# Three of a decode kernel's fourteen weights loads issued as parts of their rows

## The chip, the cores and the metric

One core of a Trainium2 chip runs the whole program. The metric is the device time of one execution in microseconds (us); the time before is 2493.15 us, the median of two runs (2493.1 and 2493.21).

## The reference

Two tokens (batch 2, one query position, width 512) go through four blocks: attention, mixer, attention, mixer, each with a residual sum around it. Both attention blocks use the same weights and the same caches.

```python
q = (x @ wq).reshape(B, Sq, 32, 128)              # 32 query heads, 8 key/value heads
scores = einsum("bhqd,bhkd->bhqk", q, k) * Dh**-0.5   # k, v: 2 x 8 x 32768 x 128 f32
o = einsum("bhqk,bhkd->bhqd", softmax(scores), v)
x = x + o.reshape(B, Sq, 4096) @ wo
h = layernorm(layernorm(x)); u = gelu(einsum("bsd,sf->bdf", h, w1) + b1)   # f = 1792
x = x + transpose(einsum("bdf,fs->bds", u, w2) + b2)
```

For one batch entry and one key/value head the keys are 16 MB and the values 16 MB. There are 16 such pairs and two layers, so nearly all the data that has to be read is the two caches, twice.

## The kernel before

The work is cut into 32 units: a layer, a batch entry and a key/value head. A unit reads its keys in eight chunks of 128 x 4096 floats (2 MB each), multiplies each by the queries into `scores` (`k_chunk`, L418), takes the maximum and the exponentials, then reads its values in eight chunks and sums them up in `acc` (`v_chunk`, L563). Small steps close the unit: denominators, the output projection into `rows` (`add_row`, L236), and after the last unit of a batch entry the mixer.

All large transfers are issued by SyncE on one queue (SP), in one order that is written out when the program is built: the list `stream`, sorted by a key that interleaves the keys of a unit with the values of the unit before. Except around the change of layers, a transfer brings four chunks, 8 MB (128 rows of 64 KB). The target is one large SBUF tile `mem`, divided into 13 cells of 128 x 4096 floats (16 KB in each of 128 partitions). Nine cells form the ring for keys and values, so a transfer is issued only when TensorE has finished with the cells it overwrites. Four cells hold weights.

The weights of a head are one row of `wqo`: for each of 128 partitions 8 KB of `wq` and 8 KB of `wo`, 2 MB in all, contiguous in HBM. `load_weights` (L113 to L115) brings them with one transfer of 128 rows of 16 KB. Fourteen such loads are made: all eight heads in the first layer (order 0, 1, 2, 3, 4, 6, 5, 7, `passing` ahead of `RESIDENT`) and again the six heads of `passing` in the second. Each is booked ten chunks ahead of its unit's first key chunk (L908, `at(kbeg[n] - 10, load_weights, ...)`); the first product that reads them (`q_products`, L330) is booked six chunks ahead of it.

Around the change of layers (roughly from 1010 to 1560 us of the span) transfers are smaller, 256 KB to 4 MB, because the units of heads 5 and 7 of both layers are interleaved with the mixer, and some chunks stay in SBUF for the second layer.

The builder gives every transfer of the two hardware queues one of eight semaphores in turn. A transfer adds to its semaphore as its data lands, and a reader waits for the semaphores of all transfers that bring what it reads.

Of the kernel before, what the change touches and what calls it, by code (L numbers as in the profile page):

```python
# [13 lines left out]
P = 128  # L14
# [21 lines left out]
DIRECT = 2  # L36
TAIL_GROUPS = (3, 3, 3, 2, 1)
IDLE = (4, 1, 3, 2)
EPS = 1e-5


@with_exitstack
def gqa_mixer_kernel(ctx: ExitStack, tc: tile.TileContext, x, kt, v, wqo, cols, out):
# [17 lines left out]
    nc = tc.nc  # L61
# [42 lines left out]
    def cells(k, m=1):  # L104
        return mem[:, k * CK : (k + m) * CK]
# [4 lines left out]
    def wo_at(h):  # L110
        return cells(home[h])[:, W:].rearrange("p (t c) -> p t c", t=R)

    def load_weights(h, cell):  # L113
        home[h] = cell
        nc.sync.dma_start(cells(cell), wqo[h])  # L115


    busy = [0] * 2 * (WCELL0 + WCELLS + 1)
# [57 lines left out]
    booked, closed = {}, {}  # L176

    load_weights(0, WCELL0)
    cols_sb = sm["cols"]
    nc.scalar.dma_start(cols_sb, cols)  # L180
# [64 lines left out]
    def first_input():  # L245
# [13 lines left out]
        nc.vector.tensor_reduce(rs, p[:, : B * DT].rearrange("p (b d) -> p b d", b=B), axis=AX.X, op=ALU.add)  # L259
        nc.vector.tensor_scalar(rs, rs, 1.0 / D, EPS, op0=ALU.mult, op1=ALU.add)  # L260
        nc.gpsimd.tensor_tensor(rs, rs, half_neg.to_broadcast([P, B]), op=ALU.pow)
# [49 lines left out]
    def unit_of(n):  # L311

        return units[n]
# [320 lines left out]
    def deviation(dst, mv):  # L634


        nc.vector.tensor_scalar(dst, mv[:, 1:2], 1.0 + EPS, EPS * EPS, op0=ALU.mult, op1=ALU.add)
        nc.gpsimd.tensor_tensor(dst, dst, half_neg, op=ALU.pow)
# [49 lines left out]
    def idle_products(k):  # L688


        p = misc()
        for _ in range(k):
            nc.tensor.matmul(p[:, :P], ident, ident, start=True, stop=True)

    def last_mixer(n):
# [21 lines left out]
        for k in range(2):  # L717
# [3 lines left out]
            nc.vector.bn_stats(st[:, k, :], halves[k][:, :w])  # L721
        idle_products(IDLE[0])
        nc.vector.bn_aggr(mv, st)
# [8 lines left out]
        for g in range(NG):  # L732
# [7 lines left out]
            )  # L740
        idle_products(IDLE[1])

        def project(f):
            for g in range(NG):
                nc.tensor.matmul(  # L745
                    kept[0][32 * g : 32 * g + 1, :P],
                    w2z[:, f, 1:],
                    tiles[f][:, g * P : (g + 1) * P],
                    start=False,
                    stop=(f == FT - 1),  # L750
                    skip_group_check=True,
                )

        for f in range(DIRECT):
# [3 lines left out]
            project(f)  # L758
        idle_products(IDLE[2])
        f0 = DIRECT  # L760
        for i, m in enumerate(TAIL_GROUPS):
# [8 lines left out]
            if i < 2:  # L770
                idle_products(IDLE[3])
            f0 += m
# [45 lines left out]
    def statistics(key):  # L818
# [3 lines left out]
        nc.vector.bn_aggr(mv, st)  # L822
        nc.vector.tensor_scalar_add(rs, mv[:, 1:2], EPS)
        nc.gpsimd.tensor_tensor(rs, rs, half_neg, op=ALU.pow)
# [43 lines left out]
    kbeg, k_done, vbeg, v_done, brings, t = {}, {}, {}, {}, [], 0  # L868
# [9 lines left out]
    def at(time, f, *a, rank=1):  # L878
        done.setdefault(time, []).append((rank, f, a))

    HC = NCH // HALVES
    weight_cell = {h: WCELL0 + h % WCELLS for h in heads}
    again = dict(zip(passing, (WCELL0 + k for k in (0, 2, 3, 1, 0, 2))))
    mixed = {}
    for n in range(NU):
        layer, b, h = unit_of(n)
# [18 lines left out]
            if place is S[0]:  # L905
                assert v_done[n - 2, HC - 1] <= q2
        if n and (units[n] == (0, 0, h) or h in passing and units[n] == (1, 0, h)):
            at(kbeg[n] - 10, load_weights, h, (again if layer else weight_cell)[h])  # L908
        if n in (N1 + 1, N2 + 1):
            at(kend - 0.5, turn_scores, n, 0, rank=2)  # L910
            at(kend, q_products, n + 1, 0)
# [157 lines left out]
```

## Time and profile before

| what | value |
|---|---|
| median of two runs | 2493.15 us |
| the profiled execution's own time | 2494.97 us |
| its span, first to last instruction | 2493.1 us |
| TensorE busy | 1378.2 us (55%) |
| VectorE busy | 240.1 us (10%) |
| ScalarE busy | 187.9 us (8%) |
| moved by DMA | 1063.04 MB, mean 426 GB/s |
| mean granted TensorE clock | 0.771 |

A page of the profile has the busy time of each engine, 40 slices of the span, the DMA queues with the share of the core's 16 DMA engines that they kept busy, the chain of work that ended last, the costliest groups of instructions with what they waited for, and the DMA issues. A table by stretches of time gives the same for chosen windows. PE is TensorE, DVE VectorE, ACT ScalarE, POOL GpSimd, SP SyncE; SPq is SP's queue of issues. No view tells the 16 DMA engines apart; their mean busy share in short stretches is what can be read.

### The profile page before, as it was taken

The page shows a single profiled execution, that of the slowest core. Times are in us where ns is not written, and L with a number is a line of the kernel's source. Part 1 is how long each engine was busy: PE and PEld are TensorE (multiplying, and loading weights), DVE is VectorE, ACT ScalarE, POOL GpSimd, SP SyncE. Part 2 cuts the span into 40 slices and gives each one's busy share as a digit, 9 for nine tenths or more (in the row PEclk, how much of TensorE's full clock was granted, in tenths as well). Part 3 has the DMA queues.
Part 4 walks back from the last instruction along what each step waited for, and adds up shares of the span by engine and source line. Part 5 has one row for each costly group of instructions (what it writes and reads, how often), then busy time and mean ns, then how long its engine had stood idle before and what let it go on. Part 6 is the DMA issues. An engine that isn't in the chain of part 4 may idle for free.

```text
span 2493.1 us, 20496 instructions
## 1 busy us (share of the span) xinstructions
PE 1378.2 (55%) x9270; PEld 369.7 (15%) x9270; DVE 240.1 (10%) x632; ACT 187.9 (8%) x554; POOL 4.9 (0%) x17
## 2 busy tenths in 40 slices
PE   4544554545445554767677665365546555455546
PEld 1111111111111111111121111111111111111112
DVE  1000000000000000003113110000000000010002
ACT  0000000000000000002012010000000000011002
POOL 0000000000000000000000000000000000000000
PEclk7777777877777777778798887777777777777778
DMA  9999999999999999999999999999999999999996
GB/s 420 436 433 424 436 436 433 430 436 433 431 429 437 433 430 431 429 426 403 428 425 421 427 430 427 435 433 428 435 433 433 430 432 432 430 436 431 431 436 282
DMA packets 34080, 1063.04 MB, mean 426 GB/s; under 512 B 4037, under 2 KB 4041, under 8 KB 4938
## 3 DMA queue, kind: packets, MB, share of 16 engines
q1 hardware_dynamic: 33704, 1061.70, 99.1%
q8 instruction: 73, 1.20, 0.2%
q14 instruction: 13, 0.11, 0.0%
q10 hardware_dynamic: 290, 0.04, 0.0%
HBM read 1061.72 MB, written 0.00 MB: 426 GB/s over the span
## 4 chain that ended last, share of the span: by engine, by line
DMA 74%; PE 24%; issue 0%; DVE 0%; ACT 0%; SPq 0%; POOL 0%
DMA mem<-in_v_dram 39%; DMA mem<-in_kt_dram 35%; PE scores L418 11%; PE acc L563 11%; PE kept L330 1%; PE rows L236 1%; PE bcast L330 1%; PE small L603 0%; PE small L447 0%; PE small L594 0%; PE kept L745 0%; PE small L441 0%; PE bcast L813 0%; PE small L356 0%; SPq L136 0%
## 5 line engine op out<-in xcount | busy, mean ns | idle before, releaser
L418 PE MATMUL scores<-mem,small_sb 128*32 128x512 f32 x4096 | 629.9, 732 | 615.9 <-DMA mem<-in_kt_dram 615.8
L563 PE MATMUL acc<-mem,S 128*16 128x512 f32 x4088 | 612.0, 735 | 454.1 <-DMA mem<-in_v_dram 454.1
L418 PEld LDWEIGHTS scores<-mem,small_sb 128*32 128x32 f32 x4096 | 147.8, 128 | 1008.8 <-issue 902.5
L458 ACT ACTIVATE S<-S,small_sb 128x128 f32<-128x128 f32 x240 | 123.5, 518 | 2103.1 <-DVE small_sb L449 1628.4
L563 PEld LDWEIGHTS acc<-mem,S 128*16 128x16 f32 x4088 | 133.3, 110 | 815.5 <-issue 674.0
L433 DVE TENSOR_REDUCE small_sb<-scores 128x1 f32<-128x512 f32 x64 | 44.2, 690 | 826.9 <-PE scores L418 826.9
L453 DVE STREAM_TRANSPOSE S<-scores 128x512 f32<-128x512 f32 x64 | 45.4, 710 | 123.6 <-PE acc L563 123.6
L330 PE MATMUL kept<-mem,small_sb 128*2 128x512 f32 x104 | 50.1, 606 | 1.7 <-DVE small_sb L264 1.7
L236 PE MATMUL rows<-mem,small_sb 128*1 128x512 f32 (+1 forms) x276 | 48.6, 617 | 2.6 <-ACT mem L788 2.4
L458 ACT ACTIVATION_READ_ACCUMULATOR S<-S,small_sb 128x1 f32 x240 | 44.8, 187 | 0.0
L443 DVE TENSOR_REDUCE small_sb<-small 1x4 f32<-1x128 f32 x32 | 8.9, 279 | 287.8 <-PE small L441 287.8
L596 DVE RECIPROCAL small_sb<-small 128x4 f32<-128x4 f32 x32 | 5.9, 184 | 291.9 <-PE small L594 291.9
L605 DVE TENSOR_TENSOR small_sb<-small,small_sb 128x4 f32<-128x4 f32 x31 | 5.1, 164 | 289.4 <-PE small L603 289.4
L533 DVE SCALAR_TENSOR_TENSOR S<-acc,small_sb,S 128x128 f32<-128x128 f32 x93 | 32.6, 351 | 3.3
L788 ACT ACTIVATE S<-bcast,small_sb 128x512 f32<-128x512 f32 x28 | 21.6, 777 | 94.2 <-DVE small_sb L657 92.1
L531 DVE TENSOR_SCALAR S<-acc,small_sb 128x128 f32<-128x128 f32 x31 | 10.8, 349 | 160.0 <-PE acc L563 160.0
L356 PE MATMUL small<-small_sb,mem 2*128 2x2 f32 x112 | 14.7, 249 | 17.9 <-DVE mem L352 17.9
L603 PEld LDWEIGHTS small<-small_sb,S 128*128 128x128 f32 x62 | 12.6, 255 | 46.4 <-issue 39.6
L330 PE MATMUL bcast<-mem,small_sb 128*1 128x512 f32 (+1 forms) x40 | 19.1, 592 | 0.0
L805 DVE SCALAR_TENSOR_TENSOR acc<-S,small_sb,acc 128x512 f32<-128x512 f32 x24 | 18.1, 754 | 2.5
L356 PEld LDWEIGHTS small<-small_sb,mem 2*128 2x128 f32 x112 | 13.5, 186 | 30.5 <-DVE mem L352 27.3
L441 PE MATMUL small<-small_sb 128*1 128x128 f32 x64 | 17.1, 362 | 0.4 <-DVE small_sb L439 0.4
(134 smaller groups left out, 266.9 us busy)
## 6 DMA issues: line engine op xcount, KB each, us to landing
mem<-in_kt_dram SPq DMA_DIRECT2D x32, 2048.0 KB, 16.4
mem<-in_v_dram SPq DMA_DIRECT2D x23, 2048.0 KB, 20.9
mem<-in_v_dram SPq DMA_DIRECT2D x9, 4096.0 KB, 32.0
mem<-in_wqo_dram SPq DMA_DIRECT2D x14, 2048.0 KB, 33.3
mem<-in_kt_dram SPq DMA_DIRECT2D x7, 4096.0 KB, 23.7
mem<-in_kt_dram SPq DMA_DIRECT2D x24, 1024.0 KB, 8.9
mem<-in_v_dram SPq DMA_DIRECT2D x21, 1024.0 KB, 8.1
mem<-in_v_dram SPq DMA_DIRECT2D x2, 1280.0 KB, 26.6
```

What stands on the lines that cost most here:

```text
L236: nc.tensor.matmul(rows[32 * g : 32 * g + b + 1, :], weights if b else weights[:, 1:], row, start=False, stop=True, skip_group_check=True,)
L330: nc.tensor.matmul(q_ps[n][:m, :], xnT[:, d, b : b + m], wq_at(h)[:, d, :], start=(d == 0), stop=(d == DT - 1),)
L356: nc.tensor.matmul(pt[:, r * m : (r + 1) * m], q_row[n][:m, r * DH : (r + 1) * DH], ident[:m, :m], start=True, stop=True,)
L418: nc.tensor.matmul(sc_ps[n, half][32 * g : 32 * g + 32, :], q, kc[k * NG + g], start=(i == 0 and k == 0), stop=(i == PACK - 1 and k == SUB ...
L433: nc.vector.tensor_reduce(mx[n][:, half : half + 1], sc_ps[n, half], axis=AX.X, op=ALU.max)
L441: nc.tensor.matmul(pm[:1, :P], mxa, ident, start=True, stop=True)
L453: nc.vector.transpose(S[half], sc_ps[n, half])
L458: nc.scalar.activation(s[:, :, h], s[:, :, h], AF.Exp, bias=neg[n][:, h : h + 1], scale=SCALE, accum_out=lsum[n][:, half, h : h + 1],)
L533: nc.vector.scalar_tensor_tensor(t, acc[:, k * DH : (k + 1) * DH], mask[:, k : k + 1], t, op0=ALU.mult, op1=ALU.add)
L563: nc.tensor.matmul(acc[32 * g : 32 * g + R * QT, :], S[half][:, col : col + R * QT], vc[q], start=(c == 0 and q < NG), stop=(c == NCH - 1 ...
L788: nc.scalar.activation(hid[key, f], px[key], AF.Gelu_apprx_tanh, bias=shift[key][:, f : f + 1], scale=slope[key][:, f : f + 1],)
L805: nc.vector.scalar_tensor_tensor(h if f == FT - 1 else acc, h, w, acc, op0=ALU.mult, op1=ALU.add)
```

## The change

The first-layer loads of heads 3, 4 and 6 come in parts: three transfers of 112, 8 and 8 rows, two of 120 and 8, and two of 112 and 16. Together they write the same rows to the same cells. The other eleven loads, those of the same heads in the second layer among them, stay whole. Four transfers are added in all. In the order of SP's instructions the parts stand where the whole load stood; the order of the other engines is the same. The first query product of each of the three heads waits for three or two semaphores in place of one, and later transfers get another of the eight semaphores.

```diff
+UNEVEN = {3: (112, 8, 8), 4: (120, 8), 6: (112, 16)}
...
-    def load_weights(h, cell):
+    def load_weights(h, cell, reloaded=False):
         home[h] = cell
-        nc.sync.dma_start(cells(cell), wqo[h])
+        p = 0
+        for m in UNEVEN[h] if h in UNEVEN and not reloaded else (P,):
+            nc.sync.dma_start(cells(cell)[p : p + m, :], wqo[h][p : p + m, :])
+            p += m
...
-            at(kbeg[n] - 10, load_weights, h, (again if layer else weight_cell)[h])
+            at(kbeg[n] - 10, load_weights, h, (again if layer else weight_cell)[h], layer > 0)
```

## The prediction

> **What bounds the kernel now.** I read the page's DMA lines first, then the chain that ended last, then a table by stretches, then the last microseconds slice by slice. From the page:
>
> ```profile
> span 2493.1 us, 20496 instructions
> DMA packets 34080, 1063.04 MB, mean 426 GB/s; under 512 B 4037, under 2 KB 4041, under 8 KB 4938
> q1 hardware_dynamic: 33704, 1061.70, 99.1%
> q8 instruction: 73, 1.20, 0.2%
> DMA 74%; PE 24%; issue 0%; DVE 0%; ACT 0%; SPq 0%; POOL 0%
> L418 PE MATMUL scores<-mem,small_sb 128*32 128x512 f32 x4096 | 629.9, 732 | 615.9 <-DMA mem<-in_kt_dram 615.8
> L563 PE MATMUL acc<-mem,S 128*16 128x512 f32 x4088 | 612.0, 735 | 454.1 <-DMA mem<-in_v_dram 454.1
> ```
>
> SP's queue q1 keeps the 16 DMA engines busy for 99.1% of the span, and both large groups of matmuls are idle for as long as they wait for its data. TensorE is no bound. The 24% of the chain on PE is not time without transfers; the table by stretches shows why (columns: busy us and counts of PE, PEld, DVE, ACT, POOL, granted clock, DMA share, GB/s):
>
> ```profile
> 60.00:380.00 320.00, 162.34 (x1114) 44.77 (x1114) 21.75 (x63) 19.34 (x72) 0.00 (x0) 0.75 1.00 433
> 380.00:720.00 340.00, 172.93 (x1190) 47.15 (x1194) 23.57 (x68) 17.21 (x64) 0.00 (x0) 0.76 1.00 433
> 720.00:1010.00 290.00, 148.43 (x995) 39.83 (x986) 19.57 (x54) 15.01 (x56) 0.00 (x0) 0.75 1.00 431
> 1140.00:1190.00 50.00, 37.60 (x234) 9.36 (x230) 24.13 (x46) 14.12 (x19) 1.09 (x2) 0.88 0.98 396
> 1560.00:2440.00 880.00, 454.87 (x3071) 123.03 (x3063) 65.92 (x184) 64.92 (x197) 0.54 (x1) 0.75 1.00 432
> ```
>
> From 60 to 1010 us the DMA share is 1.00 at 431 to 433 GB/s: the next transfer is always queued. All three changed loads lie there. An edit can move the time only by how long the DMA engines need, and a transfer has landed only when its slowest engine is done. The table is a mean over 16 engines; whether they run level shows where the queue runs dry. The end of the last transfers:
>
> ```profile
> 2470.00:2471.00 1.00, 0.85 (x8) 0.00 (x0) 0.00 (x0) 0.00 (x0) 0.00 (x0) 1.00 1.02 408
> 2471.00:2472.00 1.00, 0.32 (x4) 0.13 (x8) 0.00 (x0) 0.00 (x0) 0.00 (x0) 1.00 0.67 268
> 2472.00:2473.00 1.00, 1.00 (x16) 0.23 (x8) 0.00 (x0) 0.00 (x0) 0.00 (x0) 1.00 0.49 197
> 2473.00:2474.00 1.00, 0.59 (x8) 0.00 (x0) 0.00 (x0) 0.00 (x0) 0.00 (x0) 1.00 0.50 195
> 2474.00:2475.00 1.00, 0.88 (x8) 0.13 (x8) 0.00 (x0) 0.00 (x0) 0.00 (x0) 1.00 0.27 104
> 2475.00:2476.00 1.00, 0.78 (x20) 0.32 (x16) 0.70 (x2) 0.00 (x0) 0.00 (x0) 1.00 0.13 49
> 2476.00:2477.00 1.00, 0.72 (x19) 0.22 (x16) 0.70 (x2) 0.00 (x0) 0.00 (x0) 1.00 0.01 4
> ```
>
> The share falls from 1.0 to 0.5 within 2471 to 2472, rests there for two slices, and then falls to nothing. Read as two halves: 0.67 is 0.50 of one half and 0.17 of the other, which therefore ended about 0.34 us into its slice, at 2471.3; the second half holds 0.50 + 0.49 + 0.50 + 0.27 + 0.13 + 0.01 = 1.90 of half a share, 3.8 us, and ends at 2474.8 on the mean, 3.5 us later. So there is a fast half and a slow half. The same at the end of the first stage:
>
> ```profile
> 1146.00:1147.00 1.00, 1.00 (x9) 0.10 (x9) 0.84 (x3) 0.00 (x0) 0.00 (x0) 1.00 0.94 393
> 1147.00:1148.00 1.00, 0.35 (x2) 0.26 (x2) 0.16 (x1) 0.00 (x0) 0.00 (x0) 1.00 0.65 254
> 1148.00:1149.00 1.00, 0.63 (x8) 0.26 (x12) 0.00 (x0) 0.00 (x0) 0.00 (x0) 1.00 0.95 287
> ```
>
> About a third of the engine time is idle between 1147 and 1148 us. That is where the first stage's lead is given up, because the next issue waits for data from the slow half. The instruction packets fit as the cause: 0.2% of 16 engines over 2493.1 us is 80 us (60 to 100 by the rounding), 1.1 us for each of 73. If they fell on eight engines, the 1560 to 2440 stretch with its 24 would set those back three each, 3.3 us:
>
> ```profile
> q8 instruction: 24, 0.39, 0.2%
> ```
>
> **The change part by part.** *One row.* The 433 GB/s of the 380 to 720 row over 16 engines is 27.06 GB/s each, so a row of 16,384 bytes takes 0.605 us, and a load of 2,097,152 bytes 4.84 us, eight rows an engine. No byte is added.
>
> *Who gets the rows.* 112 rows are seven an engine, 16 rows one. Eight rows cannot reach more than eight engines. If both 8-row parts of head 3 go to the same eight, those have nine rows and the others seven; 120 rows do not go evenly into 16, and with its 8 the load of head 4 gives some engines nine, some eight and at least one fewer. Head 6 stays at eight each. What counts is the most loaded engine of the slow half:
>
> - the eight that are used again are the fast half: the slow ones lose a row with head 3 and none or more with head 4, so the end moves by -0.605 us;
> - they are the slow half: one row more with head 3 and one with head 4, +1.21 us;
> - the two 8-row parts take different halves: head 3 gives 0, head 4 lies between 0 and +0.605 us.
>
> No row of the trace says which half takes short parts. I take -0.605 us: only in that case do the rows laid on the other half cost nothing, as two rows, 1.21 us, lie within the 3.5 us that the fast half is ahead. That the slow half is the one spared is the one step here that rests on judgement. [...]
>
> *Rows that run beside others' rows.* All transfers before are of 128 rows, so no row shows what an odd number does to the engines' rate. Bounds: 0, if a row costs 0.605 us whatever stands beside it; at the other end every row of the three loads at half rate, 3 x 4.84 = 14.5 us. Below nothing is excluded, because no engine can move a row faster than at the steady 1.00 share. I take 0, as in the stretches 60 to 1010 us the rate holds at 431 to 433 GB/s with any mix of key, value and weights rows, and keep 14.5 for the range.
>
> *Four more issues on SP.* One line of the load's source (min, median and max ns of an issue), then the issues in order of time around heads 3 and 6, where they stand between a value load and the next key load:
>
> ```profile
> L115 SPq DMA_DIRECT2D mem<-in_wqo_dram x14: 397/427/1462, 0.7 to 1974.8; - x14
> ```
>
> ```profile
> 379.51 0.33 SPq L136 DMA_DIRECT2D mem<-in_v_dram  x1
> 379.89 1.00 SPq L115 DMA_DIRECT2D mem<-in_wqo_dram  x1
> 400.03 0.33 SPq L136 DMA_DIRECT2D mem<-in_kt_dram  x1
> 700.80 0.44 SPq L115 DMA_DIRECT2D mem<-in_wqo_dram  x1
> 720.93 0.33 SPq L136 DMA_DIRECT2D mem<-in_kt_dram  x1
> ```
>
> An issue takes 0.43 us (1.46 at most). Head 3's two more end near 381.8 us, at most near 384, and the next issue is at 400.03 us, held by its buffer; around head 6 the gap is 20.1 us too, and at 1.46 us each the parts still fit. Cost 0; without that gap it would be 4 x 0.43 = 1.7 us. Later transfers also wait for their semaphore's use eight issues earlier, which is long over: the load of head 3 lands 33.1 us after its issue, and with an issue some 20 us apart eight of them are over 100 us.
>
> *The first query product.* It now waits for the last of three parts. The landing of head 3's load, then its reader:
>
> ```profile
> DMA to landing us min/median/max: 33.1/33.1/33.1
> ```
>
> ```profile
> L330 PE MATMUL kept<-mem,small_sb x8: 592/592/592, 437.6 to 442.3; 128*2 128x512 f32 x8
> ```
>
> The load lands at 379.9 + 33.1 = 413.0 us and is read at 437.6 us, so 24 us of lateness are covered, more than the 14.5 of the upper bound. Behind the product on PE stand score products, which would wait with it only past that. The other two loads are booked at the same distance. Cost 0.
>
> *The sum.* -0.605 us at the end of the first stage, handed on unchanged, as everything after 1148 us starts from landings. The profiled execution took 2494.97 us for a span of 2493.1 and would take 2494.4; it stands 1.8 us over the median, 2493.15 us, from which the forecast is 2492.5 us.
>
> **The rivals.** *Parts that get in each other's way (slower).* The eight rows of a small part go to neighbouring partitions. If four of them share a way into SBUF, they take turns: four rows one behind the other, 2.42 us in place of 0.605, and an engine of the slow half standing among them loses 1.8 us which it never makes up before the queue runs dry, for its share is 1.00. Three loads at one such stall each: +5.4 us, 2498.6 us; the bounds are one stall less the row saved (+1.2, 2494.4) and the half rate, +14.5 (2507.7). It decides as soon as an engine of the slow half loses more than 0.605 us. For it speaks that the rate of 433 GB/s is so steady that something fixed limits it; against it that no stretch shows two transfers slowing each other. [...]
>
> *The slow half is the loaded one.* +1.21 us, 2494.4 us. For it speaks nothing more than for the forecast but the chance of two halves.
>
> *The change does nothing.* The short parts spread so that each half keeps its rows, or the lead is set anew after 1148 us: 2493.15 us. For it speaks the drained stretch 1140 to 1190 us with its share of 0.98; against it that a stage which starts earlier also ends earlier.
>
> **How the numbers follow.** Forecast 2492.5 us, its own range 2491.9 (one row more saved) to 2493.0: 0.44. Parts in each other's way: 0.38. Loaded slow half: 0.10. Nothing: 0.08. The range 2491.9 to 2501.0 leaves out the stalls beyond +7.8 us, a third of that rival (0.13), and some 0.04 below. All cases lie within 2% (50 us; about what a measurement of this kernel can tell from no change): faster by more 0.01, within 0.98, slower by more 0.01, for a mechanism not thought of.
>
> **What would show it.** Right: the 1560 to 2440 and 720 to 1010 rows keep 1.00 and 432 GB/s, the first dry slice comes about 0.6 us before 1147 with a share over 0.65, since the halves are nearer to each other, and the three loads in parts land no later than 33 us after issue. Wrong, by stalls: GB/s of the 380 to 720 row falls (5 us of 340 are 1.5%, some 6 GB/s), the parts land later, and the dry slice comes later than 1147 us. Wrong, by halves: the rate stays, and the dry slice is 1.2 us later and deeper than 0.65.

## The result and the profile after

The changed kernel takes 2522.53 us (median of two runs, 2520.17 and 2524.9) against 2493.15 us: ratio 1.0113, 95% interval [1.0096, 1.0129], 29.4 us slower. The prediction, 2492.5 us in a range of 2491.9 to 2501.0, missed it; its slower rival had the kind of loss right and was too small by a factor of five. The profiled execution took 2520.17 us with a span of 2518.4 us, 25.3 us longer than before.

From the page of the changed kernel, the lines that answer to those shown of before:

```profile
span 2518.4 us, 20504 instructions
DMA packets 34119, 1063.04 MB, mean 422 GB/s; under 512 B 4076, under 2 KB 4080, under 8 KB 4977
q1 hardware_dynamic: 33743, 1061.70, 99.1%
q8 instruction: 73, 1.20, 0.2%
DMA 74%; PE 24%; issue 0%; DVE 0%; ACT 0%; SPq 0%; POOL 0%
mem<-in_wqo_dram SPq DMA_DIRECT2D x2, 1792.0 KB, 41.4
```

The bytes are the same, the queue's share is still 99.1%, and only the mean rate fell, from 426 to 422 GB/s. So the engines do not wait for more work than before; the same work takes longer. The packets under 512 B rose by 39. Before, 60 to 1010 us hold 864 of them for 53 transfers issued there, all of 128 rows, and 400 to 425 us hold 32, around the whole load of head 3 and one other transfer: 16 each. In the changed kernel 48 fall between 400 and 430 us, around the parts of head 3 and one whole transfer, 39 between 569 and 595 us around those of head 4 and another, and 48 between 738 and 765 us around those of head 6 and a third. Less 16 for each whole transfer, the parts leave 32, 23 and 32, together 87 where three whole loads leave 48. They are read here as one for each engine that takes part in a transfer, which no view shows.

By stretches of time (the last two columns are DMA share and GB/s):

```profile
60.00:380.00 320.00, 162.34 (x1114) 44.88 (x1114) 21.72 (x63) 19.32 (x72) 0.00 (x0) 0.75 1.00 433
380.00:720.00 340.00, 167.38 (x1120) 44.98 (x1120) 23.46 (x67) 17.18 (x64) 0.00 (x0) 0.73 1.00 410
720.00:1010.00 290.00, 146.53 (x988) 39.71 (x988) 19.73 (x55) 14.97 (x56) 0.00 (x0) 0.75 1.00 419
1560.00:2440.00 880.00, 460.65 (x3080) 123.92 (x3080) 66.21 (x185) 64.92 (x197) 0.54 (x1) 0.75 1.00 432
```

The rate falls exactly where the changed loads lie: heads 3 and 4 in the 380 to 720 row, head 6 in the next. 340 x (433 - 410) / 433 = 18.1 us and 290 x (431 - 419) / 431 = 8.1 us make 26.1 us, about the 25.3 us by which this execution's span is longer (the rates are rounded to 1 GB/s, so each term is good to within 1 us). In the rows before 380 and after 1560 us the rates are those of before, 433 and 432 GB/s. Around head 3, in slices of 5 us, before:

```profile
405.00:410.00 5.00, 1.73 (x12) 0.44 (x16) 0.00 (x0) 0.00 (x0) 0.00 (x0) 0.50 1.04 446
410.00:415.00 5.00, 5.00 (x42) 1.32 (x38) 0.18 (x1) 0.00 (x0) 0.00 (x0) 0.84 1.12 478
415.00:420.00 5.00, 2.40 (x24) 0.47 (x16) 0.72 (x1) 0.00 (x0) 0.00 (x0) 1.00 0.97 419
```

and after:

```profile
400.00:405.00 5.00, 0.11 (x4) 0.00 (x0) 1.48 (x3) 2.11 (x8) 0.00 (x0) 0.99 0.95 383
405.00:410.00 5.00, 0.00 (x0) 0.00 (x0) 0.00 (x0) 0.00 (x0) 0.00 (x0) 0.50 0.92 216
410.00:415.00 5.00, 4.09 (x20) 0.94 (x24) 0.00 (x0) 0.00 (x0) 0.00 (x0) 0.50 1.30 236
415.00:420.00 5.00, 5.00 (x50) 1.38 (x42) 0.18 (x1) 0.00 (x0) 0.00 (x0) 0.98 0.93 213
420.00:425.00 5.00, 0.49 (x8) 0.00 (x0) 0.72 (x1) 0.00 (x0) 0.00 (x0) 1.00 0.90 383
```

For 15 us the engines are as busy as ever (0.92, 1.30 and 0.93, 1.05 on the mean) and move half: 216, 236 and 213 in place of 433 GB/s. That is the lesson of this profile: a DMA share of 1.00 did not mean here that the packets in flight moved at full rate. The missing rate over 405 to 425 us, 5 x (217 + 197 + 220 + 50) / 433, is 7.9 us for this load.

The loss is not given back. The stretches up to 1140 us hold a share of 1.00 on the mean, and the value transfer that SP issued at 1010.1 us is now issued at 1035.0. From 1040 us on, where the transfers are smaller, the first slice of 1 us with a share under 0.75 comes at 1174 us, not 1147. Ahead of that such slices say nothing: they swing in both runs, as with 0.58 at 404 us before.

```profile
1173.00:1174.00 1.00, 1.00 (x8) 0.11 (x8) 0.89 (x3) 0.00 (x0) 0.00 (x0) 1.00 0.98 410
1174.00:1175.00 1.00, 0.40 (x5) 0.30 (x2) 0.16 (x1) 0.00 (x0) 0.00 (x0) 1.00 0.71 295
```

### The profile page after: what moved, and what is told of

It is laid out like the page before. It is cut to its first block, busy times and chain, and to the rows that moved or that the text cites. A ratio compares the mean times of both kernels' runs of the same rounds, so it can differ in the third digit from the quotient of the medians.

```text
span 2518.4 us, 20504 instructions
## 1 busy us (share of the span) xinstructions
PE 1384.1 (55%) x9270; PEld 370.7 (15%) x9270; DVE 240.3 (10%) x632; ACT 187.9 (7%) x554; POOL 4.9 (0%) x17
## 3 DMA queue, kind: packets, MB, share of 16 engines
q1 hardware_dynamic: 33743, 1061.70, 99.1%
## 4 chain that ended last, share of the span: by engine, by line
DMA 74%; PE 24%; issue 0%; DVE 0%; ACT 0%; SPq 0%; POOL 0%
DMA mem<-in_kt_dram 38%; DMA mem<-in_v_dram 37%; PE scores L422 11%; PE acc L567 10%; PE kept L334 1%; PE bcast L334 1%; PE rows L240 1%; PE small L451 0%; PE small L607 0%; PE small L598 0%; PE kept L749 0%; PE bcast L817 0%; PE small L360 0%; PE small L445 0%; ACT S L462 0%
## 5 line engine op out<-in xcount | busy, mean ns | idle before, releaser
L809 DVE SCALAR_TENSOR_TENSOR acc<-S,small_sb,acc 128x512 f32<-128x512 f32 x24 | 18.1, 755 | 2.5
## 6 DMA issues: line engine op xcount, KB each, us to landing
mem<-in_wqo_dram SPq DMA_DIRECT2D x2, 1792.0 KB, 41.4
```

The costliest lines, as they stand in the source:

```text
L809: nc.vector.scalar_tensor_tensor(h if f == FT - 1 else acc, h, w, acc, op0=ALU.mult, op1=ALU.add)
```

## The experiments

My theory after the result, which no trace had shown, was that of the slower rival, made general: DMA engines that write neighbouring partitions at one time share a way into SBUF, and a part of the rows brings engines together that a transfer of all 128 rows keeps apart (shared ways). The rivals were that the loss comes from uneven row counts, from splitting as such, or from where in HBM the engines read at one time (source). Each variant is the kernel before with an edit of `load_weights`; where nothing else is said, it acts on the first-layer loads of heads 3, 4 and 6. Each was timed beside the kernel before on the same chip.

**Split by columns.**

```diff
+        for f in (0, W) if h in (3, 4, 6) and not reloaded else (None,):
+            a = slice(f, None if f is None else f + W)
+            nc.sync.dma_start(cells(cell)[:, a], wqo[h][:, a])
```

> The same three loads (heads 3, 4, 6, first layer) come as two transfers each, of all 128 rows and half of the columns (8 KB a row). Four theories. Shared ways: DMA engines that write neighbouring partitions at one time share a way into SBUF, which a transfer of all 128 rows avoids; 2493 us, within 1.5. Uneven: the loss comes from DMA engines with more rows than others; 2493 us. Splitting: each added transfer costs something; about 29 x 3/4 = 22 us more, 2515. Source: the loss comes from where in HBM the engines read at one time (7 rows of 16 KB apart in place of 4); 2493 us.

Measured: 2493.99 us beside 2494.21, ratio 1.0 [0.9991, 1.001]. Splitting costs nothing that can be measured, and neither do rows of 8 KB. Splitting falls.

**Two parts of 64 rows.** `for m in (64, 64)`, rows in order.

> The three loads come as 64 and 64 rows: four rows for each of 16 engines, but all within one half of the partitions. Shared ways: rows at about half rate, 4.84 us more for each load, about 2508 us (2503 to 2515). Uneven: rows are even, 2493 us. Splitting: three added transfers, about 2515 us. Source: blocks of four rows as in the whole load, 2493 us.

Measured: 2519.44 us beside 2494.21, ratio 1.0099 [1.0084, 1.0114], 25.2 us more, 8.4 a load. Two parts of the same size, four rows for each of 16 engines if they are spread evenly, and nearly the whole loss: uneven and source both expected none. Shared ways had the sign, but 4.84 us a load was too small.

**Only head 6, 112 and 16 rows.**

> Only head 6 in parts, 112 and 16 rows: seven and one row for each engine, so eight each as before. Shared ways: a third of the loss, about 2502 us (2500 to 2505). Uneven: no loss, 2493 us. Splitting: one of four added transfers, about 2500 us. Source: about 2502 us.

Measured: 2503.98 us beside 2494.21, ratio 1.0038 [1.0025, 1.0051], 9.8 us. In the changed kernel the two parts of this load leave 32 small packets, as many as two whole transfers. So by the reading above all 16 engines have rows of both, seven and one if they are spread evenly, and uneven row counts are not needed for the loss.

**Whole loads from spaced source rows.**

```diff
+        src = wqo[h]
+        if h in (3, 4, 6) and not reloaded:
+            flat = wqo[h : h + 2].rearrange("h p c -> (h p c)")
+            src = flat[: P * 7168].rearrange("(p c) -> p c", c=7168)[:, : 2 * W]
+        nc.sync.dma_start(cells(cell), src)
```

> The three loads stay whole, but their source rows stand 28 KB apart, so that blocks of four rows start 112 KB apart as blocks of seven 16 KB rows do (the weights of the three heads are then others than the reference's). Source: about the whole loss, 2515 to 2523 us. Shared ways, uneven and splitting: 2493 us, within 1.5.

Measured: 2494.15 us beside 2494.21, ratio 0.9998 [0.9989, 1.0008]. Source rows 28 KB apart in place of 16 cost nothing that can be measured. This speaks for the side that is written, but only for whole loads: no part of neighbouring partitions was filled from spaced source rows.

**Which partitions meet.** Two pictures of what engines share, both suppositions that no trace shows, are set against each other. Halves: all partitions below 64 share one way, and all from 64 on another. Small ways: small groups of neighbouring partitions have ways of their own. Four variants vary the rows of a part at even counts: four parts of 32 neighbouring rows; the even and the odd rows; every fourth row; and four parts of 16 neighbouring rows with one of 64. The even and the odd rows are

```diff
+        for k in range(2) if h in (3, 4, 6) and not reloaded else (None,):
+            a = slice(k, None, None if k is None else 2)
+            nc.sync.dma_start(cells(cell)[a, :], wqo[h][a, :])
```

with `range(4)` and a step of 4 for every fourth row; the others are `for m in (32,) * 4` and `for m in (16, 16, 16, 16, 64)` in order of rows.

> The three loads come as four parts of 32 neighbouring rows (0 to 31, 32 to 63, 64 to 95, 96 to 127), two rows for each of 16 engines. Halves (all partitions below 64 share what they write through, and all above): as for 64 and 64 rows, about 2519 us. Small ways (groups of four neighbouring partitions, and the same 32 further, share one way): two engines on each of eight ways throughout, half rate, 2505 to 2530 us; it does not tell the two apart, but splitting, if it mattered, would show against two parts. Nothing shared: 2493 us.

> The three loads come as two parts of 64 rows, the even and the odd ones, so that each part reaches all of the 128 partitions with the same counts as 64 and 64 rows. Halves: engines 0 to 7 stay below partition 64 and the others above, no loss, 2493 to 2496 us. Small ways: each engine has four rows of every second partition, two ways, which it shares with one other engine; half rate, 2508 to 2520 us.

> The three loads come as four parts of 32 rows, every fourth partition. Halves: no loss, 2493 to 2496 us. Small ways: two engines start on the same way, but each engine's second row is on another, so a pair falls out of step and shares only now and then; 2500 to 2513 us, less than the four parts of neighbouring rows.

> The three loads come as four parts of 16 neighbouring rows and one of 64: one row for each of 16 engines four times, then four. Halves (what is shared is one way as wide as eight engines for all partitions below 64): the same as 64 and 64 rows, 8 to 9 us a load, 2519 to 2522 us. Small ways (each group of four neighbouring partitions has one as wide as one engine): 16 rows reach four ways, so four engines share each and a row takes 2.4 us in place of 1.2; 4 x 1.8 + 2.4 us and what the neighbours lose, 13 us a load, about 2533 us.

Measured: 32 neighbouring rows 2521.04 us beside 2494.07, ratio 1.0108 [1.0093, 1.0123]; even and odd rows 2494.3 beside 2494.07, ratio 1.0001 [0.9991, 1.0011]; every fourth row 2494.33 beside 2494.07, ratio 1.0001 [0.9992, 1.0011]; 16 neighbouring rows 2522.06 beside 2495.24, ratio 1.0104 [1.0087, 1.0121]. Halves had all four about right; small ways expected a loss from both strided variants and 2533 us from the 16 neighbouring rows, and missed these three.

One pair carries the study: 64 neighbouring rows and 64 rows at every second partition have the same sizes and the same number of parts, and cost 25.2 us and nothing (2494.3 us beside 2494.07). Slices of 5 us around head 3, first with 64 and 64 neighbouring rows:

```profile
405.00:410.00 5.00, 0.00 (x0) 0.00 (x0) 0.00 (x0) 0.00 (x0) 0.00 (x0) 0.50 0.87 177
410.00:415.00 5.00, 2.63 (x16) 0.68 (x20) 0.00 (x0) 0.00 (x0) 0.00 (x0) 0.50 1.26 269
415.00:420.00 5.00, 5.00 (x42) 1.36 (x38) 0.19 (x1) 0.00 (x0) 0.00 (x0) 0.80 0.97 242
```

then with the even and the odd rows:

```profile
405.00:410.00 5.00, 1.54 (x8) 0.37 (x12) 0.00 (x0) 0.00 (x0) 0.00 (x0) 0.50 1.06 452
410.00:415.00 5.00, 5.00 (x34) 1.34 (x30) 0.04 (x1) 0.00 (x0) 0.00 (x0) 0.64 1.05 449
415.00:420.00 5.00, 3.48 (x32) 0.70 (x24) 0.86 (x2) 0.00 (x0) 0.00 (x0) 1.00 1.03 446
```

Half rate against full rate, at the same share. What decides is which rows a part takes, neighbouring or spaced, not how many rows it has or how many parts there are. The pair does not tell writing from reading: with the partitions the source rows are spaced too. The strided parts had been expected to cost something by small ways, with each engine taking rows next to each other in the list; that picture of which engine writes which rows falls with the 0.2 and 0.3 us measured.

**Each load alone.** Head 3 in (112, 8, 8) and head 4 in (120, 8).

> Only head 3 in parts, 112, 8 and 8. If the loads' losses add up, 7.5 to 8.5 us by the landings behind it in the changed kernel, about 2502 us; if the two parts of eight rows, four engines to a way, cost by themselves, more than head 6 with its 112 and 16.

> Only head 4 in parts, 120 and 8. If the losses add up, 9 to 11 us, about 2504 us, so that the three single loads (heads 3, 4, 6) sum to the 26 to 29 us of the change. If uneven rows mattered, this one, with the most uneven counts, would lose far more than head 6, whose counts are even.

Measured: head 3 2502.96 us beside 2495.24, ratio 1.003 [1.002, 1.0041], 7.7 us; head 4 2504.76 beside 2495.24, ratio 1.0038 [1.0025, 1.0051], 9.5 us. With head 6 the sum is 27.0 us, about the change's 29.4. The load supposed most uneven, head 4, does not lose more than head 6 (9.5 us beside 9.8), and head 3 with two parts of eight rows does not cost more than head 6 with one of 16 (7.7 us beside 9.8).

**How wide a way is.** `((32, 96), (0, 32), (96, P))` and `(96, 32)`.

> The three loads come as 64 rows across the middle (32 to 95), then 0 to 31 and 96 to 127. Halves (eight engines' width shared by all partitions below 64, as much above): the middle part has eight engines in either half and loses nothing, the two others run at half rate; about half of the 8.5 us a load, 2506 to 2508 us. Finer ways, where neighbouring rows of any part meet: as 64 and 64 rows, 2517 to 2522 us.

> The three loads come as 96 and 32 rows: six and two rows for each of 16 engines. Halves: two thirds of the engines are below 64 in the first part, so it runs a third slower, and the second part at half rate; 3 to 5 us a load, 2503 to 2508 us. Finer ways: 8 to 9 us a load, 2517 to 2522 us.

Measured: 64 rows across the middle 2510.65 us beside 2493.67, ratio 1.0066 [1.0049, 1.0082], 17.0 us or 5.7 a load; 96 and 32 rows 2521.51 beside 2493.67, ratio 1.011 [1.0095, 1.0125], 9.3 a load. Halves expected 4.3 and 3 to 5; finer ways 8 to 9 for both. The middle variant gains, though less than halves say (from 380 to 720 and from 720 to 1010 us it moves 420 and 422 GB/s, where 64 and 64 rows moved 412 and 420), and 96 rows lose as much as 64. Neither picture holds for both. The middle variant also bears on the source: its parts read unbroken pieces of 1, 0.5 and 0.5 MB and lose 17.0 us, while pieces of 1 and 1 MB (64 and 64 rows) lose 25.2 us and four of 0.5 MB (32 rows) 27.0. So the size of the piece read does not set the loss.

## Why the prediction was wrong, point by point

*What bounds the kernel* was right: the DMA engines do, at a share of 1.00 from 60 to 1010 us, and time lost there reaches the end. 26.1 us are lost by 1010 us and the span is 25.3 us longer.

*One row and who gets it.* The counts fit the small packets: 112 and 16 rows leave 32, as many as two whole transfers, and the loads with parts of eight rows leave fewer than 16 a part, 32 for head 3's three and 23 for head 4's two. How these fall to the parts, and which engines a part of eight rows runs on, no view shows. The term of -0.605 us, by which the forecast stands under the time before, is shown by no run. It may be there; beside losses of 7.7 to 9.8 us a load it can't be seen, and whether a row moved to another engine saves anything stays open. So does the step behind the term, a fast and a slow half of the engines with instruction packets as the cause: it was read from the end of the queue alone, and no run tests it.

*Rows that run beside others' rows* is the step that failed. The prediction took 0, "as in the stretches 60 to 1010 us the rate holds at 431 to 433 GB/s with any mix of key, value and weights rows". All of that mix was 128-row transfers, so it was no evidence for other shapes. Measured, the term is 7.7 us for head 3, 9.5 for head 4 and 9.8 for head 6, 27.0 in all: while parts of neighbouring rows are under way, the queue moves about half of 433 GB/s. The upper bound was wrong as well: "every row of the three loads at half rate, 3 x 4.84 = 14.5 us" holds for rows at half rate and for nothing beside them, and the measured 7.7 to 9.8 us a load is 1.6 to 2.0 times its 4.84. In the half-rate slices of head 3, 15 us at 216, 236 and 213 GB/s move 3.3 MB, one and a half times the 2.1 MB of the load. This would fit if rows of the transfers ahead and behind are slowed with the load's own; that the load's rows alone run at less than half rate would fit too, and no view separates them.

*The rival of parts in each other's way* had the direction right, and its price was mis-sized. It counted one stall of 1.8 us in a small part of each load, 5.4 us in all; in truth the large parts lose too (64 and 64 rows alone cost 25.2 us), for whole slices, 27 to 29 us in all. That four neighbouring rows take turns, from which the 1.8 us were worked out, was a supposition that no run shows: head 3 with two parts of eight rows lost 7.7 us and head 6 with one of 16 lost 9.8. What the runs show is a rate: 177 to 269 GB/s from 405 to 420 us with 64 and 64 neighbouring rows, and 446 to 452 with the even and the odd ones. How far over the partitions a part reaches does not settle it alone. The slice from 405 to 410 us with the 112 rows moved 216 GB/s, and 96 and 32 rows moved 414 and 417 GB/s in the rows from 380 to 720 and from 720 to 1010 us, as four parts of 32 did, though 96 rows reach over both halves. The 64 rows across the middle reach over both halves too, and with them it was 420 and 422. Which engine writes to which partitions, no view shows.

*SP's issues and the first query product* were right at cost 0. The parts of head 6 land 41.4 and 42.1 us after their issues in place of 33.5, which is inside the 24 us that were in hand, and the split by columns shows three added issues at no cost.

*What would show it* named the right sign, the falling GB/s of the 380 to 720 row, with some 6 GB/s for 5 us; it fell by 23.

Shown: the loss comes from parts that take neighbouring rows, as the queue then moves about half (213 to 236 GB/s in place of 433 around head 3); splitting by columns (2493.99 us beside 2494.21) and the spacing of the source in whole loads (2494.15 beside 2494.21) cost nothing that was seen, and the loss comes without uneven counts (9.8 us with head 6, by the reading of the small packets). Argued, not shown: that it arises where SBUF is written and not where HBM is read, and that it spreads to the transfers beside the load. Neighbouring partitions filled from spaced source rows would tell reading from writing. Not settled: which engine writes which partition of a part, and how wide what they share is. No variant beats the kernel before; the three that match it (columns, even and odd rows, every fourth row) are the ones to build on if a load has to be parted.

## What to carry to other kernels

A transfer into SBUF that covers a range of neighbouring partitions was not, in this kernel, a small version of one that covers all 128: a 2 MB load of 4.84 us so parted cost 6 to 10 us more on a queue with a share of 1.00. If a load must be parted, part it by columns, or by every second or fourth partition, which cost nothing here (2493.99 us beside 2494.21, 2494.3 and 2494.33 beside 2494.07). Before taking a steady rate as evidence, ask whether every transfer behind it had the same shape.

## What was not expected of the hardware

- Engines at a DMA share near 1.00 moved 151 to 269 GB/s in place of 433 while head 3's parts of 16, 64 or 112 neighbouring rows were under way; the lowest, 151, in the variant with 16 neighbouring rows, 405 to 410 us:

```profile
405.00:410.00 5.00, 0.00 (x0) 0.00 (x0) 0.00 (x0) 0.00 (x0) 0.00 (x0) 0.50 0.94 151
410.00:415.00 5.00, 2.10 (x12) 0.56 (x16) 0.00 (x0) 0.00 (x0) 0.00 (x0) 0.50 0.94 187
```

- From 405 to 410 us, when the 112-row part, the first in the queue, should be the one under way (no view tells the parts apart), the rate was already 216 GB/s; that it reaches 7/8 of the partitions did not help.
- Two transfers of 64 rows at every second partition run as fast as one of 128 rows: 2494.3 us beside 2494.07.
